# Windowed attention with sink keys, then a gated feed-forward: an early order written out by hand, sink values by a one-hot matmul, w_in loaded in mixed blocks, and output stores on another queue

## The chip, the cores and the metric

The kernel runs on one core of one Trainium2 chip. The metric is device time in microseconds, from the start to the end of one execution. Five engines run side by side, each through its own list of instructions: PE (matrix products), DVE (vector), ACT (activations), POOL (general purpose) and SP (here a queue that only issues transfers). They wait for each other on semaphores.

## The reference

The computation is attention in which each query sees the first 4 keys and the last 128 keys up to itself, and then a two-layer feed-forward with a gate. B = 4, H = 8, S = 768, D = 64; 3072 tokens, d_model 512, d_ff 2048; all inputs and the output are float32.

```python
scores = scale * np.matmul(q, k.transpose(0, 1, 3, 2))
keep = (pos[None, :] < 4) | ((rel >= 0) & (rel < 128))
scores = np.where(keep, scores, -1000000000.0)
a = np.exp(scores - np.max(scores, axis=-1, keepdims=True))
a = a / (np.sum(a, axis=-1, keepdims=True) + 1e-09)
x = np.matmul(a, v)                # heads side by side: 3072 x 512
h = x @ w_in                       # 3072 x 2048
g = h * (1.0 / (1.0 + np.exp(-beta * h)))
return g @ w_out                   # 3072 x 512
```

## The kernel before

**Tiling.** The tokens are cut into eight half-sequences of 384 tokens (`hb`, also `T_` in the feed-forward). Each has four units (`u`), a unit being two heads. The kernel computes in bf16 with float32 sums in the eight PSUM banks. For a half-sequence the stages are:

- loads of q, k (L510) and v into staging tiles, and casts to bf16 (`cast`, L530, through `copies`, L440 to L451: L444 on ACT, L446 on POOL, L449 on DVE);
- `T(u)`, L594: six transposes of q and k on PE (L602) into one bank, and one copy to `qkT`. From the fourth half-sequence on (`CUT` = 3) this is done by a transposing DMA (`XP`, L581);
- `SC(n)`, L657: scores of one or two tiles (L678), exponentials on ACT (L690, 128 x 1024), and masks in place on the tile `E`: L703 on POOL for the triangles, L698 on POOL or DVE for those with sink columns. `SS` (L716) computes scores against the sink keys;
- `AV(u)`, L736: products with the values (L757) and with the sink values `vS` (L746), reciprocal and scaling on DVE (L761, L763);
- `OT(u)`, L769: transposes of the result (L783) into `xT`; from `CUT` on by DMA (L777);
- `HQ(T_, m)`, L793: four matmuls with `w_in` for one of 16 column blocks of d_ff (L801), tanh on ACT (L806), gate on DVE (L808) into `g`;
- `OQ(T_, t, j)`, L815: matmuls with `w_out` for 128 tokens, 4 of the 16 blocks at a time (L821); after j = 3 the sum is copied to `osb` (L444 or L450) and stored by a DMA that SP issues (L830).

**Sink values.** `load_first` (L552) reads the first four value rows of every head with four small DMAs into `vS32`; `first_values` (L557) multiplies them with the ownership tile `own` into `vS`, one for each batch (L560).

**Weights.** `load_w(j)` (L512) loads 512 KB blocks j = 0 to 15, the first eight of w_in. A block of w_in holds 512 columns and half of the 512 rows, so a product of `HQ` needs two blocks. Blocks go through six staging slots, three of which lie in the third `g` buffer.

**Order.** `_program` builds a list of operations with their dependencies. `arrange` (L124) then plans it: it keeps a clock for each engine and always takes the operation that can start first. A group of PE instructions may pass at most two earlier ones (`SKIP` = 3). Operations with several possible engines (`any_of`) are given to the one that ends first. `resolve` puts semaphore waits where operations on different engines depend on each other. So each engine's list is fixed before the launch, and a late operation holds up all that stands behind it in the same list. The first half-sequence's order is written out (L965 to L1008), with fill matmuls on constants (L1003) where PE would otherwise stand idle; from L1009 a loop picks the next stage by what is ready first. Loads are listed in `LOADS` (L844): half-sequences 0 and 1, then all 16 weight blocks, then the others. SP issues all transfers, loads, transposes and stores, in one list.

Of the kernel before, what the change touches and what calls it, by code (L numbers as in the profile page):

```python
# [17 lines left out]
HALF = S // 2  # L18
# [4 lines left out]
class Op:  # L23
    __slots__ = ("eng", "fn", "deps", "signal", "count", "waits", "sem", "vc", "dma", "seq", "end", "ns", "alts",
                 "group", "tail", "hold", "preds", "ready", "left", "succ", "at")


class Graph:
# [7 lines left out]
    SKIP = 3  # L36
    SLACK = 0
# [16 lines left out]
    def add(self, eng, fn, ns=0, r=(), w=(), x=(), dma=None, alts=None, after=(), hold=550):  # L54
# [7 lines left out]
        o.signal, o.count, o.waits, o.vc, o.hold = False, 0, [], None, hold  # L62
# [61 lines left out]
    def arrange(self):  # L124
# [7 lines left out]
        for o in ops:  # L132
            for p in o.preds:
                p.succ.append(o)
        after = None
# [18 lines left out]
        def done(o):  # L154
            planned.add(id(o))
            new.append(o)
            for s in o.succ:
                s.left -= 1
                if s.left == 0 and s.eng != "pe":
                    pool.append(s)  # L160

        pool = [o for o in ops if o.left == 0 and o.eng != "pe"]
        while todo_pe or pool:
            best = None
            for i, grp in enumerate(todo_pe[:self.SKIP]):
# [182 lines left out]
def _program(nc, G, sb, ps, q, k, v, w_in, w_out, beta, out):  # L348
# [8 lines left out]
    maskS = sb("maskS", (128, 2, 128), BF16)  # L357
    beta_st = sb("beta_st", (16, 128), F32)
# [18 lines left out]
    vS32 = sb("vS32", (128, B, D), F32)  # L377
# [12 lines left out]
    def add(eng, fn, ns, r=(), w=(), x=(), dma=None, after=(), hold=550):  # L390
        return G.add(eng, fn, ns, r, w, x, dma, None, after, hold)
# [26 lines left out]
    held = {7}  # L418

    def choose(n):  # L420

        runs = [list(range(i, i + n)) for i in range(9 - n) if not held & set(range(i, i + n))]
        return min(((max(G.bank_at(("B", j)) for j in c), c) for c in runs), default=None)
# [8 lines left out]
    def take(n):  # L432
        got = choose(n)[1]
# [20 lines left out]
    def consts():  # L454
# [4 lines left out]
                                            base=0, channel_multiplier=-1), 150, r=["ones"], w=["ident32"])  # L459
        for i, sg in ((0, -1), (1, 1)):  # L460
# [7 lines left out]
        add("gp", lambda e: e.memset(vS32[:, :, :], 0.0), 250, w=["vS32z"])  # L468
# [7 lines left out]
        for i, sg in ((0, 1), (1, -1)):  # L476
            add("gp", lambda e, i=i, sg=sg: e.affine_select(
                maskS[:, i, :], ones[:, :], [[sg, 128]], ALU.is_ge, 0.0, base=min(sg, 0), channel_multiplier=-sg),
                250, r=["ones"], w=[("maskS0", i)])
        add("gp", lambda e: e.affine_select(maskS[:, :, :], maskS[:, :, :], [[0, 2], [0, 128]], ALU.is_ge, 1.0,  # L480
                                            base=-NSINK, channel_multiplier=1), 400,
            r=[("maskS0", 0), ("maskS0", 1)], w=["maskS"])
# [14 lines left out]
    def load(hb, n, i):  # L497

        b, t0, z = hb // 2, hb % 2 * HALF, hb % NSTG
        if n == "v" or hb >= CUT:  # L500
            src = {"q": q, "k": k, "v": v}[n][b, :, t0 + i * 128:t0 + (i + 1) * 128, :].rearrange("h p d -> p h d")
            dst, keys, ns = stg[n][z][:, i, :, :], [("stb", n, z, i)], 262144 / 240
        else:
            hs = slice(0, H) if i is None else slice(2 * i, 2 * i + 2)
# [565 lines left out]
```

## Time and profile before

| | |
|---|---|
| five executions | 230.63, 228.3, 231.03, 228.38, 231.51 us; median 230.63 |
| profiled execution: time, span | 230.63 us, 228.7 us |
| mean granted PE clock | 0.99 |
| longest instructions by group (busy us, mean ns) | L801 PE 95.1, 326; L821 PE 90.3, 379; L806 ACT 72.9, 585; L808 DVE 68.7, 550; L703 POOL 49.5, 717; L690 ACT 43.0, 1030 |
| SP, queue time of the four sink-value loads | 2.98 us, from 8.68 to 11.66 |
| SP waiting for the osb copy before a store | 31.3 us in 6 waits |
| a store, from issue to landing | 2.5 us median |
| moved by DMA in stretches of 5 us from 0 to 30 | 159, 267, 150, 324, 223, 291 GB/s |

The span is what the profile shows from the first to the last instruction; the rest of the time lies around it. Matmuls are pipelined, so their mean durations overlap: four matmuls of L801 follow each other in 0.65 us, four of L821 in 0.86 us. A line of the profile's groups gives the line of the kernel, the engine, the operation, its output and inputs, the count, then busy time and mean duration, then the idle time of that engine just before and what ended it.

### The profile page before, as it was taken

To read this page: it belongs to the slowest core of one execution; us is meant where nothing else is said; L and a number is where in the kernel's file an instruction comes from. 1 tells how busy PE (TensorE), PEld (TensorE's weight loads), DVE (VectorE), ACT (ScalarE), POOL (GpSimd) and SP (SyncE) were. 2 spreads that over 40 slices of the span, in tenths; PEclk is the share of its full clock that TensorE was granted. 3 is DMA by queue.
4 is the path that set the end of the run, shared out by engine and by line. 5 is a ranking of instruction groups with operands and counts; after the bars stand their busy time and mean duration, and the time that the engine had idled before them with its cause. 6 is when DMAs were issued, how large, how long until landed. Compare 5 with 4: busy or idle time off the path is not lost.

```text
span 228.7 us, 4562 instructions
## 1 busy us (share of the span) xinstructions
PE 214.8 (94%) x1771; PEld 124.8 (55%) x1795; DVE 139.4 (61%) x293; ACT 142.8 (62%) x226; POOL 66.0 (29%) x118
## 2 busy tenths in 40 slices
PE   8974799999999999999999999999999999999993
PEld 6662566554546556555655555656555565555541
DVE  2793469997596447557966563767765654533310
ACT  3844988765871487737667479672767764744421
POOL 6573592003361053407100047350120740000000
PEclk9999799999999999999999999999999999999998
DMA  6979799999976995967746995998769523011112
GB/s 180 236 200 332 207 357 359 341 321 237 220 150 141 242 216 86 221 165 147 155 87 162 229 207 94 216 187 171 131 127 208 185 80 83 0 46 49 47 48 89
DMA packets 95157, 39.79 MB, mean 174 GB/s; under 512 B 81808, under 2 KB 87968, under 8 KB 95136
## 3 DMA queue, kind: packets, MB, share of 16 engines
q1 hardware_dynamic: 95136, 39.51, 72.7%
q8 instruction: 14, 0.23, 0.4%
q14 instruction: 7, 0.06, 0.1%
HBM read 27.30 MB, written 6.29 MB: 147 GB/s over the span
## 4 chain that ended last, share of the span: by engine, by line
PE 82%; DMA 6%; ACT 4%; DVE 2%; SPq 2%; POOL 1%; issue 1%
PE P L801 36%; PE P L821 35%; DMA k_stage<-in_k_dram 6%; PE P L757 4%; PE P L678 4%; ACT E L690 2%; PE P L746 1%; PE P L602 1%; SPq L554 1%; ACT qkT L444 1%; POOL E L703 1%; SPq L510 1%; DVE w_in L449 1%; DVE g L808 1%; PE P L783 1%
## 5 line engine op out<-in xcount | busy, mean ns | idle before, releaser
L806 ACT ACTIVATE t<-P,hbeta 128x384 f32<-128x384 f32 x128 | 72.9, 585 | 39.3 <-PE P L801 31.1
L808 DVE SCALAR_TENSOR_TENSOR g<-t,P 128x384 bf16<-128x384 f32 x128 | 68.7, 550 | 45.9 <-ACT t L806 42.8
L801 PE MATMUL P<-xT,w_in 128*128 128x384 bf16 x512 | 95.1, 326 | 0.7 <-ACT E L690 0.5
L821 PE MATMUL P<-w_out,g 128*128 128x512 bf16 x360 | 90.3, 379 | 1.7 <-issue 0.6
L703 POOL TENSOR_SCALAR_AFFINE_SELECT E<-E 128x512 bf16<-128x512 bf16 x72 | 49.5, 717 | 77.0 <-ACT E L690 76.8
L801 PEld LDWEIGHTS P<-xT,w_in 128*128 128x128 bf16 x512 | 48.3, 98 | 37.4 <-DVE w_in L449 0.9
L821 PEld LDWEIGHTS P<-w_out,g 128*128 128x128 bf16 x384 | 36.5, 98 | 36.4 <-DVE w_out L449 0.3
L690 ACT ACTIVATE E<-P 128x1024 bf16<-128x1024 f32 x44 | 43.0, 1030 | 10.0 <-PE P L678 9.7
L444 ACT ACTIVATE osb<-P 128x512 f32<-128x512 f32 x19 | 11.4, 599 | 20.3 <-PE P L821 19.6
L763 DVE TENSOR_TENSOR onorm<-P,rden 128x384 bf16<-128x384 f32 x32 | 17.8, 556 | 1.0
L757 PE MATMUL P<-vaug,E 128*128 128x65 bf16 x352 | 17.1, 193 | 0.2 <-POOL E L703 0.2
L757 PEld LDWEIGHTS P<-vaug,E 128*128 128x128 bf16 x352 | 15.6, 97 | 2.4 <-POOL E L703 0.3
L678 PE MATMUL P<-qkT 64*128 64x128 bf16 (+1 forms) x288 | 14.8, 235 | 0.7 <-ACT ES L720 0.4
L678 PEld LDWEIGHTS P<-qkT 64*128 64x128 bf16 x288 | 9.7, 96 | 8.3 <-issue 2.6
L746 PE MATMUL P<-vS,ES 128*128 128x130 bf16 x64 | 12.8, 220 | 1.4 <-DVE vS L560 1.0
L449 DVE CAST k<-k_stage 128x512 bf16<-128x512 f32 (+1 forms) x19 | 9.6, 510 | 6.0 <-DMA k_stage<-in_k_dram 6.0
L761 DVE RECIPROCAL rden<-P 128x6 f32<-128x6 f32 x32 | 6.0, 188 | 10.4 <-PE P L757 10.3
L449 DVE CAST vaug<-v_stage 128x512 bf16<-128x512 f32 x21 | 9.9, 476 | 3.6 <-DMA v_stage<-in_v_dram 3.3
L446 POOL TENSOR_SCALAR_AFFINE_SELECT q<-q_stage 128x512 bf16<-128x512 f32 x6 | 4.3, 730 | 25.3 <-DMA q_stage<-in_q_dram 25.2
L1003 PE MATMUL P<-ones 128*128 128x256 bf16 x54 | 9.5, 321 | 1.1 <-POOL ones L455 1.1
L444 ACT ACTIVATE qkT<-P 128x768 bf16<-128x768 bf16 x9 | 7.0, 810 | 5.4 <-PE P L602 5.4
L449 DVE CAST q<-q_stage 128x512 bf16<-128x512 f32 (+1 forms) x15 | 7.1, 473 | 5.3 <-DMA q_stage<-in_q_dram 5.3
(50 smaller groups left out, 94.7 us busy)
## 6 DMA issues: line engine op xcount, KB each, us to landing
v_stage<-in_v_dram SPq DMA_DIRECT2D x24, 256.0 KB, 4.6
out_dram<-osb SPq DMA_DIRECT2D x24, 256.0 KB, 2.5
q_stage<-in_q_dram SPq DMA_DIRECT2D x15, 256.0 KB, 4.8
k_stage<-in_k_dram SPq DMA_DIRECT2D x15, 256.0 KB, 4.9
wst<-in_moe_w_in_dram SPq DMA_DIRECT2D x5, 512.0 KB, 9.2
wst<-in_moe_w_out_dram SPq DMA_DIRECT2D x4, 512.0 KB, 4.6
g<-in_moe_w_out_dram SPq DMA_DIRECT2D x4, 512.0 KB, 5.2
q_stage<-in_q_dram SPq DMA_DIRECT2D x2, 768.0 KB, 6.0
```

The lines of the kernel that those rows point to most:

```text
L444: return lambda e: e.activation(dst, src, AF.Copy, bias=0.0, scale=scale)
L449: return lambda e: e.tensor_copy(dst, src)
L678: add("pe", lambda e, dst=dst, kt=kt, kc=kc, rows=rows, q0=q0, nq=nq, u=u: e.matmul(dst, kt[rows, kc:kc + 128], qkT[rows, u % NT, 0, q0:q0 ...
L690: add("act", lambda e, src=src, dst_=dst_: e.activation(dst_, src, AF.Exp, bias=0.0, scale=SCALE), act_ns(1024), w=[("E", z)] + [("m", z, ...
L703: add("gp", lambda e, dd=dd, sg=sg: e.affine_select(dd, dd, [[0, 4], [sg, 128]], ALU.is_ge, 0.0, base=min(sg, 0), channel_multiplier=-sg), ...
L746: add("pe", lambda e, m=m, c0=c0: e.matmul(A[:, c0:c0 + 2 * (D + 1)], ES[u // 4 % 2][:, m * 128:(m + 1) * 128], vS[b % 2][:, 2 * hp:2 * hp ...
L757: e.matmul(A[:, c0:c0 + D + 1], E[t_ % NE][:, i, hh, :], vaug[vz][:, kb % NK, 2 * hp + hh, :], start=a, stop=o, skip_group_check=True), 31,
L763: add("dve", lambda e: e.tensor_tensor(onorm[on][:, :, :, :].rearrange("p m h d -> p (m h) d"), av[:, :, 0:D], rden[on][:, :].unsqueeze(2) ...
L801: add("pe", lambda e, c=c: e.matmul(hp, w_in16[:, c, m * 128:(m + 1) * 128], xT[:, c, t0:t0 + HALF], start=(c == 0), stop=(c == 3)), mm_ns ...
L806: add("act", lambda e: e.activation(tt[ti][:, :], hp, AF.Tanh, bias=0.0, scale=hbeta[:, m:m + 1]), act_ns(HALF) + 93, r=["hbeta"], w=[("t" ...
L808: add("dve", lambda e: e.scalar_tensor_tensor(gt[T_ % NG][:, m, :], tt[ti][:, :], 1.0, hp, ALU.add, ALU.mult), dve_ns(HALF), r=[("t", ti)] ...
L821: add("pe", lambda e, m=m: e.matmul(P[:, bk, :], gt[T_ % NG][:, m, t * 128:(t + 1) * 128], w_out16[:, m, :], start=(m == 0), stop=(m == NM ...
```

## The change

- **Sink values.** For the first batch a matmul takes the place of the loads: a constant one-hot tile `sel` picks the first four rows of the first v block, for all heads (`first_values_pe`), and the multiplication with `own` then reads PSUM. For each later batch one DMA reads 16 rows of v (`load_first`), placed among the later loads.
- **w_in.** A block now holds 256 columns and all 512 rows, so one block serves two products of `HQ`. Weight blocks come before q and k of the second half-sequence: `LOADS` is half-sequence 0, w0, w1, w2, q, w3, k, w4, w5, v, then w6 to w15. The first casts are bound to an engine.
- **Loads of the first half-sequence.** q and k come in three transfers each in place of four. SP's order of the early loads is fixed by a chain. Beta is loaded behind w1.
- **The early order.** Transposes, scores, attention of the first half-sequence, then products H0 to H10 mixed with transposes and scores of the second, are written out with their PSUM banks. q and k of the first eight units get a bank and a copy each. PE groups may pass nine others while PE's planned time is under 60 us.
- **Masks.** The triangles of the first two half-sequences may also be applied by DVE, with `maskT`.
- **First output products.** For `T_` = 0 the order is j outside, t inside, with three banks held.
- **Stores.** All output stores but those of the last half-sequence are issued by POOL; the plan books 1000 ns of POOL for each.

```diff
+    WIDE, EARLY = 10, 60000
...
-            for i, grp in enumerate(todo_pe[:self.SKIP]):
+            for i, grp in enumerate(todo_pe[:self.SKIP if self.free["pe"] > self.EARLY else self.WIDE]):
...
-            src = w_in_src[:, 2 * h:2 * h + 2, m * 512:(m + 1) * 512]
+            src = w_in_src[:, :, j * 256:(j + 1) * 256]
...
+        any_of(copies(dst, src_, {"act": 947} if j == 0 else {"gp": 1060} if j < 3 else {"act": 947, "dve": 602, "gp": 1060}), r=[("wst", j % NWS)], w=[("w16", m, h)])
...
-        add("sp", lambda e: e.dma_start(vS32[s_:128:16, :, :], v[:, :, s_, :].rearrange("b h d -> h b d")), 60,
-            r=["vS32z"], w=[("vS32", s_)], dma=f"ds{s_}")
+        add("sp", lambda e: e.dma_start(vS32[:, 0, :], v[b, :, 0:16, :]), 100,
+            w=["vS32"], dma="ds")
...
+    def first_values_pe():
+        G.begin()
+        bk = take(1)
+        add("pe", lambda e: e.matmul(P[:, bk[0], :], sel[:, :], vaug[0][:, 0, :, 0:D], start=True, stop=True), mm_ns(512),
+            r=["sel", ("v", 0, 0)], x=[("B", bk[0])])
+        add("dve", lambda e: e.tensor_tensor(
+            vS[0][:, :, 0:D], P[:, bk[0], :].rearrange("p (h d) -> p h d", d=D),
+            own[:, :].unsqueeze(2).to_broadcast([128, H, D]), ALU.mult), dve_ns(H * D),
+            r=["own", ("vSo", 0)], w=[("vS", 0)], x=[("B", bk[0])])
+        give(bk)
...
-        bs = take(1)
+        bs = take(1) + (take(1) if hb < 2 else [])
...
+        if len(bs) == 2:
+            for i in range(2):
+                mp = P[:, bs[i], :].bitcast(BF16)[:, i * HALF:(i + 1) * HALF]
+                any_of(copies(qkT[:, u % NT, i, :].rearrange("p (s j) -> p s j", j=NK),
+                              mp.rearrange("p (j s) -> p s j", j=NK), {"dve": 470, "act": 380}),
+                       w=[("qkT", u % NT, i, c) for c in range(NK)], x=[("B", bs[i])])
...
+                    if TILES[t_][0][1] < 8:
+                        alts["dve"] = (lambda e, dd=dd, tri=tri: e.tensor_tensor(dd, dd, tri, ALU.mult), 335)
...
-            add("sp", lambda e: e.dma_start(out_t[3 * T_ + t], osb[z][:, :]), 262144 / 300, r=[("osb", z)],
-                dma=f"do{z}")
+            eng = "gp" if T_ < NSB - 1 else "sp"
+            add(eng, lambda e: e.dma_start(out_t[3 * T_ + t], osb[z][:, :]), 262144 / 300, r=[("osb", z)],
+                dma=f"do{eng}{z}", hold={"sp": 550, "gp": 1000, "act": 600}[eng])
...
-    LOADS = xl(0) + xl(1) + list(range(16)) + [x for hb in range(2, NSB) for x in xl(hb)]
+    x1 = xl(1)
+    LOADS = xl(0) + [0, 1, 2] + x1[:1] + [3] + x1[1:2] + [4, 5] + x1[2:] + list(range(6, 16))
+    LOADS += [("f", 1)] + [x for hb in range(2, NSB) for x in xl(hb) + ([("f", hb // 2 + 1)] if hb in (3, 5) else [])]
...
-    OS = [(T_, t, j) for T_ in range(NSB) for t in range(3) for j in range(4)]
+    OS = [(0, t, j) for j in range(4) for t in range(3)]
+    OS += [(T_, t, j) for T_ in range(1, NSB) for t in range(3) for j in range(4)]
...
+    for x in "T0 T1 S0 T2 S1 T3 S4 S2 V S3".split():
+        if x == "V":
+            cast(0, "v", 0)
+            first_values_pe()
+        else:
+            {"T": T, "S": SC}[x[0]](int(x[1:]))
...
+    for name, i in [("A", 0), ("A", 1), ("R", 0), ("A", 2), ("R", 1), ("A", 3), ("R", 2), ("R", 3)]:
+        step(name, i)
...
+    early = "H0 H1 H2 H3 H4 H5 T4 T5 T6 T7 H6 S5 H7 H8 S6 H9 S7 H10".split()
+    for x in early:
+        if x == "H0":
+            beta_in()
...
+        step(x[0], int(x[1:]))
```

In this code "A" stands for `AV`, "R" for `OT`, "H" for `HQ`, "S" for `SC` and "gp" for POOL.

## The prediction

> **What bounds the kernel now.** I read the busy shares first, then the span in slices, the windows by stage, the timeline of the first 30 us, the chain of waits, and last the queues of POOL and SP.
>
> ```profile
> PE 214.8 (94%) x1771; PEld 124.8 (55%) x1795; DVE 139.4 (61%) x293; ACT 142.8 (62%) x226; POOL 66.0 (29%) x118
> PE   8974799999999999999999999999999999999993
> POOL 6573592003361053407100047350120740000000
> ```
>
> PE is the bound; the row of tenths shows that it is full from the sixth slice (28.6 us) to the last. So only the front can give much. Windows over the whole program, then over the fill matmuls of L1003 alone (start:end, length, PE busy, then the other engines):
>
> ```profile
> 0.00:4.40 4.40, 3.35 (x16) 2.34 (x17) 0.64 (x2) 1.49 (x2) 3.45 (x22) 1.00 0.50 147
> 4.40:18.90 14.50, 12.37 (x157) 8.82 (x155) 12.05 (x26) 8.89 (x12) 8.13 (x13) 1.00 0.91 239
> 18.90:28.40 9.50, 5.68 (x71) 3.89 (x68) 3.31 (x7) 6.55 (x10) 4.08 (x6) 0.82 0.91 255
> 28.40:35.00 6.60, 5.98 (x72) 4.05 (x73) 4.44 (x10) 5.55 (x10) 6.60 (x10) 1.00 1.03 360
> 35.00:60.00 25.00, 24.30 (x171) 14.25 (x171) 22.54 (x46) 17.97 (x34) 2.79 (x6) 1.00 1.05 303
> ...
> sum 28.40, PE 9.48 PEld 5.61; mean PE 3.16 PEld 1.87
> ```
>
> Up to 28.4 PE is busy 21.4 us, 9.5 of them filler: only 11.9 us are work, 16.5 us are not. Between 35 and 190 it idles 0.70 + 0.31 + 0.48 + 0.79 = 2.3 us. What the front waits for is in the chain of waits in order of time, and on PE's timeline:
>
> ```profile
> 9.17 0.57 SPq L554
> 12.19 9.15 DMA k_stage<-in_k_dram
> 15.00 0.22 PE L746 MATMUL P<-vS,ES 128*128 128x130 bf16 x1 [1.01 <-DVE vS L560]
> 18.73 0.34 PE L783 MATMUL P<-ident,onorm 128*128 128x128 bf16 x3
> 21.85 0.75 PE L602 MATMUL P<-ident,k 128*128 128x128 bf16 x3 [2.61 <-DVE k L449]
> 28.48 1.47 PE L801 MATMUL P<-xT,w_in 128*128 128x384 bf16 x8 [0.52 <-ACT E L690]
> ```
>
> Four sink-value loads hold SP at 8.7 to 11.7; the second half-sequence's k is issued behind them and takes 9.15 us; PE stands still for it; the first product with w_in starts at 28.48, though the last transpose of its input was done near 19.1.
>
> **The early order.** Three steps bring the first xT forward. (a) The sink rows come through a one-hot matmul from v's first block (at the price of the 512-column matmul in the chain, 0.86 us for 4: 0.2 us) instead of DMAs; the 1.01 us wait at 15.00 goes. (b) DVE ran L560 twice there (2.15 us, 13.74 to 15.89), the second for another batch, ahead of the first reciprocal at 15.81; that second 1.1 us goes to a later place, and about 0.5 us with it. (c) q and k of each unit get two PSUM banks: one ACT copy of 810 ns becomes two of about 485 (ACT's 384-column xT copy), +0.16 us of engine time for each of eight units, beside other work. So xT is ready at 19.1 - 1.5 = 17.6 us. The two small operations for the one-hot tile add 0.45 us to POOL at the start and a memset of 0.30 goes; POOL has about 2 us free at 4 to 6. What is late next is w_in.
>
> SP queue: the 2.98 us of L554 and beta's 0.47 go from the front, eight q/k loads become six (1.0 us less). Loads for the sink rows of later batches return as one DMA each (about 0.5 us of SP), after the weights. Beta's load stands behind the second w_in load; its transpose (0.23 us PE, 0.17 us DVE) now stands just before the first tanh, which waits if beta is late; it has some 8 us to land and took 3.4.
>
> Data: ahead of the third w_in load lie 2.36 + 1.57 = 3.9 MB. By the stretches of 5 us, before had moved 0.80, 2.13, 2.88, 4.50, 5.62, 7.07 MB at 5, 10, ... 30 us. It had moved 3.9 MB by 18.2, with a hole at 10 to 15 (150 GB/s) that closes when L554 goes. One w_in load now serves two products of 0.65 us (16 matmuls in 2.60 us), so products H0 to H5 can run from 17.6 to 21.5. Only the first is sure to find its weights early; a miss costs under 1 us. Their casts are now bound to engines: the first to ACT (0.63 for half as many columns: about 1.1), two to POOL (1.05 each), both with idle time at 15 to 21. While PE is in its first 60 us, a group that is ready may pass up to nine others in place of two, so H6 and H7 can come forward into the gap before k. The row length of a w_in load falls from 2 KB to 1 KB, which no row here shows: below by nothing, above by the v loads' 256-byte rows (239 GB/s in the window where they run, against 360 from 28.4 on: 0.7 us for each of eight, 5.8 in all). I take nothing, as q's 768-byte rows make up most of the 324 GB/s at 15 to 20.
>
> Against it, three weight loads (1.57 MB) and w_in's fourth now precede k of the second half: 6.0 MB up to k. Hole closed, 5.1 MB at 20 us and then 0.31 MB per us: 23 us, against 21.3 (earliest 22; without the gain 26.4). That half's chain is 1.7 us later.
>
> Gain by that limit: eleven products, 11 x 0.65 = 7.15 us of PE work, done in time idle before, less 1.7: 5.4 us. A second limit is ACT: each product wants one L806 (0.585), and the six exponentials (1.03 each) have no other engine. From 17.6 to 35 ACT was busy 12.7 us (0.6, then 6.55 and 5.55 in the two windows), idle 4.7. The split copies put 4 x 0.485 on it for the second half's units in place of 3 x 0.81: 0.5 freed. Leave 1.7 for the gap between H7's end (22.8) and the first copy behind k (24.5): (4.7 + 0.5 - 1.7) / 0.585 = 6 products more than before by 35, 3.9 us of PE. This one ends last: I take 3.9, between 2 and 6.5.
>
> The rest of the front: masks of the first two halves may go to DVE (0.40 us on L698, against 0.72 on POOL). At 28.4 to 35 POOL is full and PE idles 0.62; I take 0.4 gained. The T_=0 output products in the order j outside, t inside hold three banks in place of one; the next scores, which want five of eight, come near 60 us. Nothing, covered by that order; if it failed, a score burst would wait for 3 x 0.86 us.
>
> **The stores.** 21 of 24 leave SP for POOL. On SP L830 costs 0.56 us each and waits 31.3 us; behind it stand loads and both DMA transposes. But PE idles only 2.3 us in 35 to 190, so the freed queue is worth 0 to 1: nothing, nearest to the rows of PE waits, which hardly name these transfers. On POOL each store waits for its osb copy, and queued behind are the masks, for which L757 waits. POOL is busy 41.0 of 130 us between 60 and 190:
>
> ```profile
> L703 POOL TENSOR_SCALAR_AFFINE_SELECT E<-E 128x512 bf16<-128x512 bf16 x54 | 36.3, 701 | 73.9 <-ACT E L690 73.7
> L757 PE MATMUL P<-vaug,E 128*128 128x65 bf16 x352 | 17.1, 193 | 0.2 <-POOL E L703 0.2
> ```
>
> A POOL store's issue is not in the trace: nearest row SP's (0.56, longest 1.42); the kernel's own plan books 1.0 for it; the Trainium skill, "DMA: Bandwidth & Descriptors", section Specifications, puts the first byte at about 1 us. I take 1.0: 21 us of POOL, 62 of 130. PE's wait for masks, 0.5 us now with the loads before it, may double: 0.5 us of loss, between -1 (freed SP) and 8.
>
> Here a rule speaks against the change. In the trace POOL's masks run 632 ns at best and 1085 at worst, DVE's casts 416 and 853: the two engines hold each other up by at most 0.45 us. "SBUF — State Buffer", section "A bandwidth-pool intuition that's wrong (but worth ruling out)", says that a DMA issued by GpSimd is held until the DVE copy ends, about 3100 ns in place of 620. DVE casts from SBUF fill 18.3 of the 130 us (14%), so three stores meet one: by the rule 3 x 2.5 = 7.5 us on POOL, a third of it (POOL's busy share) on PE, 2.5 us; by the row 3 x 0.45 / 3 = 0.5. I take the row, which fits casts of 0.43 us.
>
> Sum: -3.9 - 0.4 + 0.2 (sink matmul) + 0.5 = -3.6 us. The profiled execution took 230.63 us (span 228.7 and 1.9 around it), which is also the median of the five runs: 227.0.
>
> **The rivals.**
> - *The front is bound by its transfers.* DMA is at 0.91 to 1.05 in the windows from 4.4 to 60 us, and the order only permutes the same 13.1 MB (4.7 of q, k, v, 8.4 of weights). If k lands at 26.4, 7.15 - 5.1 = 2.0 us are gained, and the 1 KB rows can eat that: 228.6 to 231, say 230. Against it: the hole at 10 to 15.
> - *Stores on POOL hold the masks.* At 60 to 190 masks come in bursts of 2.4 us. If each store that meets a busy POOL (32%) passes its 1.0 + 0.43 us to PE, less 0.2 of planned slack, 21 x 0.32 x 1.23 = 8.3 us: 227.0 - 0.5 + 8.3 = 234.8, slower. It decides from 4.1 + 2.3 = 6.4 us, or 0.30 us a store. For it: POOL E L703 is in the chain at 105.9. Against: one such wait in 130 us.
> - *The front fills fully.* If DVE takes more copies and ACT is no limit, 6.5 us in place of 3.9: 224.4.
>
> **How the numbers follow.** Two us or so (1%) can't be told from no change; the five runs lie between 228.3 and 231.5. The likeliest case 0.52 (224.5 to 229.3, of which 0.06 within 1%), front fully filled 0.11, transfer-bound 0.20 (within 1%), masks held 0.17. Faster 0.57, same 0.26, slower 0.17. The range 222.5 to 231.5 leaves out the held masks and little below.
>
> **What would show it.** L801 starting near 17.6; the first k of the second half landing near 23; ACT nearly full from 24 to 35; PE idle small after. L703 waiting for stores, or L757 for L703 more than 1 us in all, would show the masks held. I am wrong if w_in is late at 17.6, or if POOL's stores take over 1.5 us each.

## The result and the profile after

| | before | after |
|---|---|---|
| median | 229.69 us (227.41 to 232.83, 80 runs) | 228.61 us (226.89 to 230.35, 43 runs) |
| profiled execution: time, span, granted clock | 230.63, 228.7 us, 0.990 | 228.21, 226.3 us, 0.998 |

The ratio of after to before is 0.9965, with the interval [0.9947, 0.9983]: about 0.8 us faster, where 3.6 were forecast. (Medians are of all runs; the ratios leave out runs more than 1.5% above the fastest of their kernel.) The two profiled executions differ by 2.4 us, more than the medians do; the profile of before fell on a run with a lower clock. So the profiles serve here for the where, the ratios for the how much.

The page of after, busy shares and the rows of tenths:

```profile
PE 213.8 (94%) x1762; PEld 122.4 (54%) x1787; DVE 141.3 (62%) x299; ACT 147.0 (65%) x237; POOL 71.3 (32%) x131
...
PE   8797978999999999999999999999999999999994
...
POOL 6263154016350266047000564073100570000000
```

PE's hole at the third to fifth slice (7, 4, 7 before) is nearly gone (9, 7, 9), and a shallow dent (7, 8) has come behind it, at 28 to 40 us. Windows of after, with the same columns as before:

```profile
4.40:18.90 14.50, 11.70 (x146) 7.93 (x143) 10.44 (x25) 9.93 (x16) 6.78 (x12) 1.00 0.97 279
18.90:28.40 9.50, 8.66 (x66) 4.71 (x64) 7.61 (x17) 8.24 (x18) 1.32 (x2) 1.00 1.05 320
28.40:35.00 6.60, 5.04 (x83) 3.21 (x82) 6.49 (x13) 6.48 (x9) 3.50 (x5) 1.00 0.94 289
35.00:60.00 25.00, 23.94 (x184) 13.87 (x185) 20.51 (x42) 15.32 (x26) 6.99 (x12) 1.00 1.10 312
```

From 18.9 to 28.4 PE is busy 8.66 us, none of it filler, in place of 5.68. From 28.4 to 35 it idles 1.56 us in place of 0.62, with ACT (6.48 of 6.60) and DVE (6.49) full; from 35 to 60 it idles 1.06 in place of 0.70.

To see when work is won and lost, I count the matmuls of each kind up to a time, weigh each with its spacing in a burst (0.16 us for one of `HQ`, 0.22 for one of `OQ`, and so on) and take the difference to before. I call it the lead. Some matmul records are missing, so it is good to about half a us, and it drifts later.

| lead over before, us, at | 20 | 25 | 30 | 35 | 40 | 45 | 60 |
|---|---|---|---|---|---|---|---|
| after | 0.1 | 3.1 | 3.9 | 2.6 | 0.7 | 1.0 | 1.6 |

The 3.9 us that were forecast for the early order are there at 30 us, and 3.2 of them are gone at 40. PE's timeline of after shows the stretch (start, length, instruction, and in brackets the idle time before and what ended it):

```profile
19.61 5.96 PE L860 MATMUL P<-xT,w_in 128*128 128x384 bf16 x32
25.40 0.33 PE L649 MATMUL P<-ident,q 128*128 128x128 bf16 x3
...
28.42 0.62 PE L733 MATMUL P<-qkT 64*128 64x256 bf16 x14
...
30.99 0.39 PE L733 MATMUL P<-qkT 64*128 64x256 bf16 x6 [0.52 <-ACT E L745]
31.90 0.40 PE L733 MATMUL P<-qkT 64*128 64x128 bf16 x8 [0.52 <-ACT E L745]
32.81 0.40 PE L733 MATMUL P<-qkT 64*128 64x256 bf16 x6 [0.52 <-ACT E L745]
...
38.70 0.82 PE L860 MATMUL P<-xT,w_in 128*128 128x384 bf16 x4 [0.59 <-DVE g L867]
```

Eight products run back to back from 19.61 (28.48 before). Then come the transposes of the second half-sequence, at 25.40 (the first of k at 21.85 before), since its k landed late, as POOL's timeline shows:

```profile
24.68 0.66 POOL L473 TENSOR_SCALAR_AFFINE_SELECT k<-k_stage 128x512 bf16<-128x512 f32 x1 [2.91 <-DMA k_stage<-in_k_dram]
```

From 30 us PE is paced by ACT: each group of scores waits until an exponential frees its banks. ACT's timeline of after, and then of before:

```profile
28.52 0.58 ACT L865 ACTIVATE t<-P,hbeta 128x384 f32<-128x384 f32 x1 [0.29 <-PE P L860]
29.00 3.76 ACT L745 ACTIVATE E<-P 128x1024 bf16<-128x1024 f32 x4
32.62 0.52 ACT L779 ACTIVATE ES<-P 128x384 bf16<-128x384 f32 x1
32.99 0.62 ACT L865 ACTIVATE t<-P,hbeta 128x384 f32<-128x384 f32 x1
33.45 1.99 ACT L745 ACTIVATE E<-P 128x1024 bf16<-128x1024 f32 x2
```

```profile
25.18 1.03 ACT L690 ACTIVATE E<-P 128x1024 bf16<-128x1024 f32 x1
26.09 0.51 ACT L720 ACTIVATE ES<-P 128x384 bf16<-128x384 f32 x1
26.46 4.72 ACT L690 ACTIVATE E<-P 128x1024 bf16<-128x1024 f32 x5
```

The second half's six exponentials end at 35.4 in place of 31.2. Its masks, values and transposes all follow later by about as much, and until then PE has little else, since most of the early products are behind it: from 30 to 40 us it idles 2.5 us (0.5 before).

The stores, from the groups of after (see the prediction for the same rows of before):

```profile
L759 POOL TENSOR_SCALAR_AFFINE_SELECT E<-E 128x512 bf16<-128x512 bf16 x64 | 42.9, 692 | 61.3 <-ACT E L745 60.8
L890 POOL DMA_DIRECT2D out_dram<-osb x21 | 12.1, 579 | 51.7 <-ACT osb L471 51.7
L816 PE MATMUL P<-vaug,E 128*128 128x65 bf16 x352 | 17.2, 193 | 1.5 <-DVE E L753 0.7 <-DVE E L763 0.3 <-POOL E L759 0.3
```

A store costs POOL 0.58 us (at most 0.78). Masks on POOL wait for exponentials, not for stores, and PE waited 0.3 us for a POOL mask.

### The profile page after: what moved, and what is told of

It reads as the page before. It is cut to its first block, busy times and chain, and to the rows that moved or that the text cites. A ratio compares the mean times of both kernels' runs of the same rounds, so it can differ in the third digit from the quotient of the medians.

```text
span 226.3 us, 4534 instructions
## 1 busy us (share of the span) xinstructions
PE 213.8 (94%) x1762; PEld 122.4 (54%) x1787; DVE 141.3 (62%) x299; ACT 147.0 (65%) x237; POOL 71.3 (32%) x131
## 4 chain that ended last, share of the span: by engine, by line
PE 76%; DVE 11%; ACT 4%; DMA 3%; POOL 1%; issue 1%; SPq 1%
PE P L880 34%; PE P L860 33%; PE P L816 4%; PE P L733 3%; DMA k_stage<-in_k_dram 3%; ACT E L745 3%; DVE g L867 2%; DVE E L763 2%; PE P L805 1%; DVE vaug L476 1%; DVE onorm L822 1%; DVE E L753 1%; DVE w_in L476 1%; POOL E L759 1%; SPq L541 1%
## 5 line engine op out<-in xcount | busy, mean ns | idle before, releaser
L865 ACT ACTIVATE t<-P,hbeta 128x384 f32<-128x384 f32 x128 | 73.9, 583 | 47.9 <-PE P L860 42.3
L867 DVE SCALAR_TENSOR_TENSOR g<-t,P 128x384 bf16<-128x384 f32 x128 | 70.1, 551 | 48.5 <-ACT t L865 45.0
L860 PE MATMUL P<-xT,w_in 128*128 128x384 bf16 x512 | 96.6, 326 | 0.9 <-DVE g L867 0.6
L759 POOL TENSOR_SCALAR_AFFINE_SELECT E<-E 128x512 bf16<-128x512 bf16 x64 | 42.9, 692 | 61.3 <-ACT E L745 60.8
L890 POOL DMA_DIRECT2D out_dram<-osb x21 | 12.1, 579 | 51.7 <-ACT osb L471 51.7
L471 ACT ACTIVATE osb<-P 128x512 f32<-128x512 f32 x21 | 12.6, 598 | 13.7 <-PE P L880 13.7
L753 DVE TENSOR_TENSOR E<-E,maskS 128x512 bf16<-128x512 bf16 x16 | 9.3, 588 | 5.1 <-ACT E L745 5.1
L1071 PE MATMUL P<-ones 128*128 128x256 bf16 x45 | 8.7, 342 | 1.1 <-POOL ones L482 1.1
L476 DVE CAST vaug<-v_stage 128x512 bf16<-128x512 f32 x18 | 8.9, 496 | 0.0
```

The lines of the kernel that those rows point to most:

```text
L471: return lambda e: e.activation(dst, src, AF.Copy, bias=0.0, scale=scale)
L476: return lambda e: e.tensor_copy(dst, src)
L759: alts = {"gp": (lambda e, dd=dd, sg=sg: e.affine_select(dd, dd, [[0, 4], [sg, 128]], ALU.is_ge, 0.0, base=min(sg, 0), channel_multiplier= ...
L860: add("pe", lambda e, c=c: e.matmul(hp, w_in16[:, c, m * 128:(m + 1) * 128], xT[:, c, t0:t0 + HALF], start=(c == 0), stop=(c == 3)), mm_ns ...
L865: add("act", lambda e: e.activation(tt[ti][:, :], hp, AF.Tanh, bias=0.0, scale=hbeta[:, m:m + 1]), act_ns(HALF) + 93, r=["hbeta"], w=[("t" ...
L867: add("dve", lambda e: e.scalar_tensor_tensor(gt[T_ % NG][:, m, :], tt[ti][:, :], 1.0, hp, ALU.add, ALU.mult), dve_ns(HALF), r=[("t", ti)] ...
```

## The experiments

The candidates were: that the stores on POOL took the gain; that k of the second half comes too late behind three weight loads; that DVE is full of masks; that q and k in three transfers hold up the first half; that the old gap in PE's work brings a lower clock, and filling it is what pays; and later, that ACT, DVE or the late beta is the limit at 30 to 40 us. Each ratio below is to runs of before taken beside it, with 6 to 22 runs of each kernel tried. The kernels of e1, e9, e10 and e5 keep the planned order; the others are planned anew, which can shift work elsewhere.

The PE clock that is granted in a run matters too: runs in which it dips are longer (see the last section). So the tables also give the median of those runs alone whose mean clock was 0.997 or more, with their number. For before that is 228.4 us (104 runs, 228.3 to 228.6 in each measurement). This column was worked out afterwards and has no interval.

**Parts of the change alone.**

Stores back on SP, all else kept (`e1_stores_on_sp`):

```diff
-    G.arrange()
+    G.arrange(); [setattr(o, "eng", "sp") for o in G.ops if o.dma and o.dma.startswith("dogp")]
```

> The changed kernel, with its plan kept (PE, DVE, ACT in the same order) and its 21 stores emitted by SP at the planned places. Theory 1 (the early gain of 4 us is given back between 30 and 40 us, where the second half's attention runs late; stores cost nothing): the same as the changed kernel, 0.995 to 0.998 of before, and the same PE work done at 30 and 40 us. Theory 2 (stores on POOL took the gain): some 3 us faster than the changed kernel, 0.983 to 0.986. Against both: slower than the changed kernel by 1 us or more, if SP's list needs to be free of stores.

Only the stores on POOL, in the kernel before (`e6_before_pool_stores`):

```diff
-            add("sp", lambda e: e.dma_start(out_t[3 * T_ + t], osb[z][:, :]), 262144 / 300, r=[("osb", z)],
-                dma=f"do{z}")
+            eng = "gp" if T_ < NSB - 1 else "sp"
+            add(eng, lambda e: e.dma_start(out_t[3 * T_ + t], osb[z][:, :]), 262144 / 300, r=[("osb", z)],
+                dma=f"do{eng}{z}", hold={"sp": 550, "gp": 1000}[eng])
```

> The kernel before with the stores of all but the last half-sequence issued by POOL, nothing else of the change (the planner makes its own order after it). Theory 1 and 4 (stores are worth nothing either way): 0.997 to 1.003 of before. Theory 2 (they cost some 3 us): 1.010 to 1.016. If a free SP list is worth something: 0.990 to 0.996.

Only the one-hot matmul for the sink values, in the kernel before (`e7_before_sink_matmul`), and then both of these (`e12_sink_pool_stores`, whose diff is the sum):

```diff
...
-    LOADS = xl(0) + xl(1) + list(range(16)) + [x for hb in range(2, NSB) for x in xl(hb)]
+    LOADS = xl(0) + xl(1) + list(range(16)) + [("f", 1)] + [x for hb in range(2, NSB) for x in xl(hb) + ([("f", hb // 2 + 1)] if hb in (3, 5) else [])]
...
-        if n_ == 10:
-            for s_ in range(NSINK):
-                load_first(s_)
...
-    for c in range(NK):
-        cast(0, "v", c)
+    cast(0, "v", 0)
+    first_values_pe()
+    cast(0, "v", 1)
+    cast(0, "v", 2)
```

> The kernel before with one part of the change alone: the sink values by the one-hot matmul and one later DMA for each other batch. It takes the 2.98 us of four small loads out of SP's list ahead of the second half's q and k. Theory 1 (what counts at the front is when the second half's attention gets k): k lands near 18.5 in place of 21.3, PE's gap before it nearly closes, the lead in PE work at 40 us is 2 us or more and is kept: 0.986 to 0.993, better than the whole change. Rival (the first product needs the early weights, so this part alone gives little): 0.995 to 0.999.

> The kernel before with the sink values by the one-hot matmul (alone 1.002, with a lead of 2.3 us at 40 us that was lost again, 1.2 us of it at 170 to 190 us, where a v load and transposes stood behind stores in SP's list) and the stores on POOL. If the stores in SP's list are what takes the lead back late: 0.989 to 0.994. If the lead is lost for other reasons (the planner's new order, PE's clock): 0.998 to 1.003.

| kernel | median, us | ratio, interval | clock 0.997 and up, us (runs) | lead at 30, 40 us |
|---|---|---|---|---|
| after | 228.61 | 0.9965 [0.9947, 0.9983] | 228.3 (23) | 3.9, 0.7 |
| e1: all but the stores | 229.36 | 0.9992 [0.9963, 1.002] | 228.8 (12) | 3.9, 0.9 |
| e6: only the stores | 229.53 | 0.9978 [0.9948, 1.0009] | 227.7 (7) | (low clock at 20 to 35) |
| e7: only the sink matmul | 229.77 | 1.0022 [0.9987, 1.0057] | 229.4 (9) | 2.2, 2.3 |
| e12: sink matmul and stores | 227.72 | 0.9953 [0.9927, 0.9978] | 227.5 (14) | 2.7, 2.8 |

The stores on POOL take nothing: e6 is not slower than before, and after is not slower than e1. Rather, everything but the stores (e1) brings nothing measurable. And the two small parts by themselves, in the old order of loads and work, do about as well as the whole change by the ratio, and better among the runs at the full clock, where after is not told from before. e7 missed both of its forecasts and e12 lies between its two.

What the stores cost on SP is seen late in e1, where PE is busy 14.3 of 15 us at 170 to 185 (14.9 in after). SP's timeline, then DVE's:

```profile
169.32 2.57 SPq L632 DMA_TRANSPOSE qkT<-q  x2
171.94 2.20 SPq L541 DMA_DIRECT2D v_stage<-in_v_dram  x3
174.18 7.04 SPq L890 DMA_DIRECT2D out_dram<-osb  x2
```

```profile
175.46 0.43 DVE L476 CAST vaug<-v_stage 128x512 bf16<-128x512 f32 x1 [2.64 <-DMA v_stage<-in_v_dram]
```

In SP's one list the last v loads stand behind transposes, and between these stood three stores at 150.1, 158.2 and 160.9 us. They were issued at 171.9, in after at 167.9. DVE's next instruction is a cast of that v; it waits 2.64 us, a gate stands behind it, and a score group on PE waits 0.57 us for the gate. In e7 the same place costs more: PE is busy 13.3 of 15 us there (14.7 in e12). A store stands in SP's list behind transposes until 172.18, so ACT's copy of the next sum into `osb` waits for it, and scores on PE wait for the copy:

```profile
174.64 0.60 ACT L445 ACTIVATE osb<-P 128x512 f32<-128x512 f32 x1 [1.23 <-DMA out_dram<-osb]
```

```profile
175.29 0.35 PE L732 MATMUL P<-qkT,kS 128*32 128x384 bf16 x4 [0.43 <-ACT osb L445]
```

That fits e7's lead of 2.3 at 40 us ending in no gain, and e12's lasting. It is not shown to be all of it: e7 and e12 are planned anew, and before, with its stores on SP too, is busy 14.7 of the same 15 us.

e12 also shows the other order at the front. PE's timeline:

```profile
18.58 0.74 PE L618 MATMUL P<-ident,k 128*128 128x128 bf16 x3 [0.76 <-DVE k L450]
...
20.26 0.79 PE L694 MATMUL P<-qkT 64*128 64x256 bf16 x14
...
22.55 0.82 PE L817 MATMUL P<-xT,w_in 128*128 128x384 bf16 x4 [0.58 <-ACT E L706]
```

Without the four sink-value DMAs, and with k ahead of the weights, the second half's k is transposed at 18.58 and its first scores run at 20.26 (28.42 in after). The first product comes at 22.55, three us later than in after, and the lead at 30 us is 2.7 in place of 3.9. But nothing is given back.

**What takes the lead at 30 to 40 us.** k of the second half ahead of the third w_in load (`e2_k_before_w2`); q and k of the first half in four transfers (`e4_four_loads`); both (`e8_k_early_four_loads`):

```diff
-    LOADS = xl(0) + [0, 1, 2] + x1[:1] + [3] + x1[1:2] + [4, 5] + x1[2:] + list(range(6, 16))
+    LOADS = xl(0) + [0, 1] + x1[:2] + [2, 3, 4, 5] + x1[2:] + list(range(6, 16))
```

```diff
-            hs = slice(0, H) if i is None else slice(2 * i, 2 * i + 2) if i < 2 else slice(4, H)
+            hs = slice(0, H) if i is None else slice(2 * i, 2 * i + 2)
...
-        return [(0, n, i) for i in range(3) for n in "qk"] + [(0, "v", c) for c in range(NK)]
+        return [(0, n, i) for i in range(4) for n in "qk"] + [(0, "v", c) for c in range(NK)]
...
```

> The changed kernel with q and k of the second half loaded ahead of the third and fourth w_in blocks (1.05 MB earlier for k). Theory 1: k lands some 3 us earlier than 24.7 (near 21.5), the second half's scores start near 25.5 in place of 28.4, the lead in PE work at 40 us rises from 0.7 to 2 or 3 us, and the time falls by 1 to 2 us: 0.988 to 0.993 of before. Theory 2 (stores): no change, 0.995 to 0.998. Theory 3 (DVE is full from 25 to 45 by the masks it took over): little, 0.994 to 0.998.

> The changed kernel with q and k of the first half in four transfers each, two heads in each, as before. The third unit's transposes waited for k at 10.4 us, 2.3 us later than before. If the transfer of four heads is what holds them, they come near 9, the first product with w_in starts near 18.3 in place of 19.6, and, by theory 1, little of that is kept, since k of the second half is two issues (1 us) later: 0.993 to 0.998 of before. If the start alone counts: 0.990 to 0.993.

> The changed kernel with both edits that helped alone: q and k of the second half ahead of the third w_in block (0.992), and four transfers each for q and k of the first half (0.992). If they act on two different waits in one chain (first half's transposes, then the second half's k), they add up in part: 0.985 to 0.990. If both only feed the stretch of 30 to 40 us where ACT runs the exponentials back to back, no more than one of them: 0.991 to 0.994.

Triangle masks on POOL only (`e3_masks_on_pool`: the condition `< 8` becomes `< 0`):

> The changed kernel with the triangle masks of the first two half-sequences on POOL alone, as in the kernel before. Theory 3: DVE falls below full at 30 to 40 us, the lead at 40 us rises by 1 us or more, 0.989 to 0.993 of before. Theory 1 (the late k and the exponentials on ACT set that stretch): within 0.3% of the changed kernel, 0.994 to 0.999, as the exponentials stay back to back.

More work on one engine, the orders kept. On ACT (`e9_act_more`), three of the second half's exponentials run a second time into a buffer that is free then; on DVE (`e10_dve_more`), four casts of w_in do (`extra` is set for blocks 3 to 6):

```diff
-            add("act", lambda e, src=src, dst_=dst_: e.activation(dst_, src, AF.Exp, bias=0.0, scale=SCALE),
...
+            two_ = (t_ - 5) // 2 if t_ in (5, 7, 9) else None; add("act", lambda e, src=src, dst_=dst_, two_=two_: [e.activation(o_, src, AF.Exp, bias=0.0, scale=SCALE) for o_ in ([] if two_ is None else [osb[two_][:, :].bitcast(BF16).rearrange("p (s h w) -> p h s w", s=4, h=2)]) + [dst_]][-1],
...
```

```diff
-    def copies(dst, src, ns, scale=1.0):
+    def copies(dst, src, ns, scale=1.0, extra=[]):
...
-                return lambda e: e.tensor_copy(dst, src)
+                return lambda e: [e.tensor_copy(o_, src) for o_ in extra + [dst]][-1]
...
```

> The changed kernel, every order kept, with three of the second half's six exponentials run once more into unused room (3 x 0.92 = 2.8 us more on ACT between 29 and 34 us). If ACT sets the end of the front (theory 1), 2 to 2.8 us are added to the time of the changed kernel: 1.005 to 1.009 of before. If DVE sets it (theory 3), ACT has room behind it: less than 1 us, 0.997 to 1.001.

> The changed kernel, every order kept, with the DVE casts of four w_in blocks run once more into unused room (4 x 0.68 = 2.7 us more on DVE between 22 and 35 us). If DVE sets the end of the front (theory 3): 2 to 2.7 us more, 1.005 to 1.008 of before. If ACT does (theory 1): less than 1 us more, 0.997 to 1.001. If both are in the chain in turn: 1 to 2 us more in both runs.

| kernel | median, us | ratio, interval | clock 0.997 and up, us (runs) | first product at | lead at 30, 40 us |
|---|---|---|---|---|---|
| after | 228.61 | 0.9965 [0.9947, 0.9983] | 228.3 (23) | 19.61 | 3.9, 0.7 |
| e2: k earlier | 227.48 | 0.9923 [0.989, 0.9956] | 227.1 (15) | 18.66 | 4.6, 2.0 |
| e4: four transfers | 227.54 | 0.9922 [0.9896, 0.9947] | 227.5 (12) | 17.77 | 4.2, 1.0 |
| e8: both | 227.64 | 0.99 [0.9858, 0.9941] | 227.6 (2) | 18.00 | 5.3, 1.7 |
| e3: masks on POOL | 229.2 | 0.9964 [0.9931, 0.9996] | 228.5 (7) | | |
| e9: ACT +2.8 us | 231.03 | 1.0074 [1.0045, 1.0103] | (0) | | |
| e10: DVE +2.7 us | 230.12 | 1.0028 [1.0001, 1.0054] | 230.1 (9) | | |

An earlier k pays 0.0042 of the time, about 1.0 us, and four transfers as much, both at the edge of the intervals; together they are not told apart from either alone. e4 went against the theory that little of an earlier start is kept. (Its one profile does not show its gain at 40 us, so where it comes from stays argued.)

Work added to ACT comes out as (1.0074 / 0.9965 - 1) x 228.6 = 2.5 of 2.8 us, work added to DVE as 1.4 of 2.7. So both engines count in that stretch, but which counts more is not shown, as the clock has a share in it: in e9's profile it dips before the added work begins (0.68 at 20 to 25 us) and again at 35 to 40 us, and none of e9's 17 runs kept it at 0.997. Among the runs between 0.9905 and 0.997 after has 229.1 us (21 runs), e10 230.1 (8) and e9 230.7 (7); that is 1.1 us for DVE and 1.6 for ACT, across different measurements.

The masks are not the cause. This is e3 in the window of the loss:

```profile
30.00:35.00 5.00, 3.03 (x39) 1.93 (x40) 2.20 (x4) 5.00 (x8) 4.57 (x7) 0.90 0.91 292
```

DVE falls to 2.20 of 5 us (4.95 in after), and PE is no better off, since ACT is still full at 5.00.

**The clock.** 22 more fill matmuls in the gap of the kernel before, its orders unchanged (`e5_before_fill`):

```diff
-                        self.filler = (self.WARM, self.filler[1])
+                        self.filler = (self.WARM if grp[0].group <= self.fill_to - 4 else 65, self.filler[1])
...
```

> The kernel before, every engine's order kept, with 22 more fill matmuls on PE ahead of the second half's first transposes, where PE stood still for 2.6 us and the granted clock fell to 0.76 and 0.90 in the next 10 us. Theory 4 (the executions of the kernel before differ by that fall of the clock: of 75, those with a mean clock of 0.997 and more took 228.3 us at the median, those under 0.9905 took 230.8): nearly all executions keep the full clock, and the median falls to about 228.3: 0.994 to 0.997 of before, with no earlier work at all. If the clock is no cause but only goes with something else: no change, 0.998 to 1.003; if the fill delays the transposes: slower, up to 1.003 to 1.006.

Measured: 230.3 us, ratio 1.0042 [1.0014, 1.007], the branch in which the fill delays the transposes. In its profile the first cast of k begins at 19.66 us, but the transposes wait until the fill ends, at 21.72; and the dip of the clock comes at 28 to 31 us instead. At a mean clock of 0.997 and up e5 takes 229.8 us (14 of its 22 runs), before beside it 228.4 (25 of 51). So filling the gap does not pay; what before would gain without the dip was not tested.

**With k early, what is next?** In e8 PE stands still for beta, whose load had come behind q and k. PE's timeline of e8:

```profile
21.23 0.23 PE L520 MATMUL P<-ident,beta_st 16*128 16x16 f32 x1 [0.85 <-DMA beta_st<-in_moe_beta_dram]
```

ACT's first tanh is at 21.70 there, 3.7 us behind the first product. Three edits on e8: casts of w_in and of the second half on POOL and DVE in place of ACT (`e11_casts_on_pool`); beta ahead of the first w_in load (`e13_beta_first`); both (`e15_beta_casts_pool`). And on e13, the exponentials earlier in the list (`e14_exps_first`):

```diff
-        any_of(copies(dst, src_, {"act": 947} if j == 0 else {"gp": 1060} if j < 3 else {"act": 947, "dve": 602, "gp": 1060}), r=[("wst", j % NWS)], w=[("w16", m, h)])
+        any_of(copies(dst, src_, {"act": 947} if j == 0 else {"gp": 1060} if j < 6 else {"act": 947, "dve": 602, "gp": 1060}), r=[("wst", j % NWS)], w=[("w16", m, h)])
...
-        ns = {"act": 413, "dve": 400} if hb == 0 and n != "v" else {"act": 540, "dve": 340, "gp": 612}
+        ns = {"act": 413, "dve": 400} if hb == 0 and n != "v" else {"dve": 340, "gp": 612} if hb == 1 else {"act": 540, "dve": 340, "gp": 612}
```

```diff
-        if x == 2:
+        if x == 0:
```

```diff
-    early = "H0 H1 H2 H3 H4 H5 T4 T5 T6 T7 H6 S5 H7 H8 S6 H9 S7 H10".split()
+    early = "H0 H1 H2 H3 T4 T5 T6 T7 S5 S6 S7 H4 H5 H6 H7 H8 H9 H10".split()
```

> The kernel with k ahead of the third w_in block and four transfers for the first half (0.990), with work taken from ACT and DVE in the front: the casts of w_in blocks 3 to 5 bound to POOL, which is free for 8 of 10 us at 20 to 30, and no q or k cast of the second half on ACT (2 x 0.62 us). If ACT's and DVE's load at 20 to 38 us is what gives the early lead back, 0.5 to 1.5 us less: 0.984 to 0.988 of before. If it is the chain of exponentials alone, which starts no earlier: 0.988 to 0.992.

> The kernel of e8 (k of the second half early, four loads of q and k), with beta's load issued ahead of the first w_in block. In e8 ACT stood idle for 3.38 us until beta had landed (first tanh at 21.38). Theory A: that idle time is what takes 3 us of the lead back between 30 and 40 us, since ACT then has its tanhs and the second half's exponentials in one list; then the lead at 40 us rises from 1.7 to 3 or more and the ratio to before is 0.980 to 0.987. Theory B: the scores and exponentials of the second half end as late as before whatever the tanhs do, because they wait for k and their own chain: ratio 0.987 to 0.993, lead at 40 us 1.5 to 2.3.

> The kernel of e13, with the early list changed: after H0 to H3 the transposes T4 to T7 and the scores S5 to S7, then H4 to H10. Theory A (tanhs in front of and between the exponentials on ACT delay the second half's attention): its scores end earlier, AV of the second half starts 1 us or more earlier, lead at 40 us 1 us above that of e13, ratio 0.978 to 0.986. Theory B (what is saved on one side is lost on the other: PE waits for k with H4 to H7 not yet allowed): lead at 25 us lower by 2 us, ratio as e13 or up to 0.008 above it.

> The kernel of e11 (e8 with six of the first w_in casts off ACT and DVE) with beta's load issued ahead of the first w_in block. If ACT was held by beta and by casts together, the lead at 40 us is 3 or more and the ratio 0.978 to 0.985, below that of e13; if casts play no part, as e13 within 0.002.

Then, on e13, work taken from DVE: the second half's triangle masks (`e16_beta_masks_pool`: `< 8` becomes `< 4`), its four casts of v (`e17_beta_v_pool`, below), both (`e18_beta_both_pool`):

```diff
+        if n == "v" and hb == 1:
+            ns = {"gp": 612}
         any_of(copies(dst, src, ns), r=r, w=w)
```

> The kernel of e13, with the triangle masks of the second half-sequence on POOL alone. In e13 ACT has 2.7 us free between 30 and 40 us, DVE is busy 9.9 of 10, POOL 4.3, and PE waits for DVE (gates, casts, masks). Theory A (with ACT relieved, DVE is the next limit): DVE falls by about 2 us in 25 to 40 us, PE's waits there by 1 us or more, ratio 0.980 to 0.986. Theory B (the masks go from a full DVE to a POOL that takes 0.7 in place of 0.43 for each, the same end): ratio 0.987 to 0.993, as e13.

> The kernel of e13, with the four casts of the second half-sequence's v (0.43 each on DVE) on POOL, which is idle there. Theory A (DVE is the next limit): ratio 0.982 to 0.987, and the PE waits for DVE's cast of v (0.6 at 31) are gone. Theory B: as e13, 0.987 to 0.992.

> Both edits of e16 and e17. Theory A: DVE relieved by some 4 us between 25 and 40 us, lead at 40 us 3.5 or more, ratio 0.978 to 0.985. Theory B: POOL becomes the limit there or the gain is none: 0.987 to 0.995.

| kernel | median, us | ratio, interval | clock 0.997 and up, us (runs) | lead at 30, 40 us |
|---|---|---|---|---|
| e11: e8, casts off ACT | 227.56 | 0.9897 [0.987, 0.9923] | 227.1 (12) | 4.8, 1.5 |
| e13: e8, beta first | 227.08 | 0.9886 [0.9837, 0.9935] | 226.1 (3) | 5.0, 2.8 |
| e15: e11, beta first | 226.81 | 0.9894 [0.9843, 0.9945] | 226.3 (4) | 5.2, 3.5 |
| e14: e13, exponentials first | 228.01 | 0.9933 [0.9903, 0.9964] | 227.5 (11) | 4.8, 2.4 |
| e16: e13, masks on POOL | 229.1 | 0.9984 [0.996, 1.0008] | 228.3 (9) | 5.3, 3.3 |
| e17: e13, v casts on POOL | 226.75 | 0.9882 [0.984, 0.9924] | 226.6 (5) | 5.2, 1.6 |
| e18: both | 231.48 | 1.0084 [1.0045, 1.0123] | (0) | 5.1, 3.2 |

Beta first takes ACT out of the way, as the windows of e13 show:

```profile
30.00:35.00 5.00, 3.33 (x65) 2.63 (x66) 4.97 (x10) 4.66 (x7) 4.32 (x5) 1.00 0.96 327
35.00:40.00 5.00, 4.28 (x38) 2.42 (x36) 4.90 (x13) 2.60 (x4) 0.00 (x0) 1.00 1.05 407
```

ACT is busy 7.3 of 10 us, DVE 9.9, and PE still idles 2.4; the longest waits in PE's timeline there are for DVE (a cast of v, a gate):

```profile
31.10 0.27 PE L816 MATMUL P<-vaug,E 128*128 128x65 bf16 x3 [0.56 <-DVE vaug L476]
...
33.02 0.23 PE L805 MATMUL P<-vS,ES 128*128 128x130 bf16 x1 [1.11 <-DVE g L867]
```

The lead at 40 us is 1 us higher than e8's, but a part of that is the clock: the profiles of e8, e11 and e17 have 0.71 to 0.84 at 35 to 40 us. By the ratio, too, beta's share is not told apart from nothing. e14 was a miss: a lower lead at 40 us and a ratio no better, so running the exponentials ahead of the tanhs does not help. e11 and e15 against e8 and e13 show no gain from moving the casts. Nor does e17; but DVE stays as full as in e13 there (9.9 of 10 us at 30 to 40), so it did not relieve DVE.

e16 and e18 were meant to name DVE as the next limit and do not. Their lead at 40 us is 0.4 to 0.5 above e13's, within the error of that count, and yet they are 1% and 2% slower. The reason in e16 lies far from the edit, at 90 to 100 us:

```profile
90.00:100.00 10.00, 7.25 (x72) 3.58 (x73) 8.20 (x14) 6.95 (x10) 5.56 (x8) 1.00 0.85 162
```

PE idles 2.75 us there, where e13 idles nothing: the planner, starting from other times, put three groups of scores behind each other with no product between. They wait 0.28, 0.52 and 0.52 us for exponentials, and the next output product but one waits 1.18 us for a gate. e18 loses in the same place (PE is busy 7.11 of 10 us at 90 to 100). So whether DVE is the next limit stays open, and e16 and e18 measure a replanned middle, not masks.

What beats both kernels: e17, e13, e15, e11 and e8 all lie at 0.988 to 0.990, 1% under before, with intervals that overlap.

## Why the prediction came out as it did

The range (222.5 to 231.5) holds 228.6, and the sign was right. The size was not: 0.8 us in place of 3.6. And the sign was luck: what was to bring the gain brought nothing that can be measured (e1), and what there is goes with the stores, which were booked as a loss, or with fewer dips of the clock. Neither sign of being wrong that the prediction named came: no product waited for w_in at the start, and no store took POOL over 1.5 us. Of what it expected to see, "PE idle small after" failed.

- **The early order, 3.9 us: the term that failed.** It was the ACT limit, "6 products more than before by 35, 3.9 us of PE". Measured alone with the other front parts (e1) it is 0.0008 of the time, 0.2 us [-0.5, 0.8]. The products were done early (lead 3.9 at 30 us), so the first half of the step stands. What failed is that a lead by 35 us was booked as time saved at the end. A product done early is worth something only if PE has other work at the time from which it was taken. For the late k the forecast left 1.7 us of ACT idle, but it still counted the six exponentials as done by 35 us and put what follows them at nothing. They ended at 35.4 in place of 31.2, behind a k that landed at 24.65 in place of 21.3, and the second half's masks and values came later with them; PE then idled 2.5 us at 30 to 40 us (0.5 before), and 3.2 of the 3.9 us were gone. That the late k has a part is shown by e2, about 1.0 us; that ACT and DVE have one, by e9 and e10. The rest is not shown: e2, with its early k and no dip of the clock there, still falls from 4.6 to 2.0 us.
- **k at 23.** The bytes moved by 20 us were right (5.1 MB). But when k landed, 0.8 MB more had gone than the 6.0 MB up to it (6.81 MB in after), and in before some 0.9 MB: bytes of loads that were issued behind it. A landing time reckoned from the bytes ahead alone was too early here.
- **xT ready at 17.6, first product there.** It was 19.61. The SP time of the sink values was freed as forecast. But the third transfer of q and k now holds four heads: k of unit 2 landed 6.50 us after its issue, and its transposes began at 10.36 (8.08 before). The prediction counted six loads in place of eight as 1.0 us of SP saved, and not that half the heads now wait for the larger one. With four transfers (e4) the first product is at 17.77.
- **Masks on DVE, 0.4 us.** None seen: e3 without them is at 0.9964, the change at 0.9965; the intervals (0.7 us and more) could hide 0.4.
- **Sink matmul, 0.2 us of loss.** It was costed as a matmul. What it frees in SP's list brings k forward instead (transposed at 18.58 in e12): with the stores moved too it carries a gain of the size of the whole change's, alone (e7) none.
- **Stores on POOL, 0.5 us of loss.** Each took 0.58 us in place of 1.0, and PE waited 0.3 us for masks. By e6 they gain 0.5 us [-0.2, 1.2], by after against e1 0.6; neither is clear of nothing alone, but with e12 against e7 they point the same way. So "the freed queue is worth 0 to 1: nothing" was probably the wrong end of its own bounds. SP's list matters at 170 to 185 us, where a late v load holds DVE; PE's wait rows name the gate there, not the transfer. The rival with masks held fell.
- **The row against the rule of the Trainium skill's "SBUF — State Buffer".** The row was right to take. A store's issue at most 0.78 us (median 0.56) leaves no room for issues held for some 3 us. By its section "A bandwidth-pool intuition that's wrong (but worth ruling out)" the hold ends with the DVE copy, so with casts of 0.43 us the 2.5 us a store were more than the rule makes of this case. Whether a cast held up any store's transfer no run here shows.
- **The transfer-bound rival, 230.** Its number is near, and the order of loads has a part (e2). But k landed at 24.65, not 26.4, and what PE waited for last there was ACT behind it.

Not shown: what takes 2 us of e13's lead between 30 and 40 us, and what of the change's other parts (mixed blocks, wider passing, j outside t) does anything; these were not tried singly.

## What to carry to other kernels

Work that is pulled forward into an idle stretch shortens the program only if the engine has other work where it used to stand. Before booking a gain, list what remains for that engine behind it, and when that becomes ready; here the loads for the early work went ahead of the load on which the next stage hung. And in a kernel whose lists are planned as a whole, a local edit can lose 1% elsewhere: look at the whole span before blaming the edit.

## What the runs showed of the hardware

- **The granted clock goes with the time from run to run.** Of 75 runs of the kernel before that were measured with e1 to e4, 32 had a mean clock of 0.997 or more and a median of 228.3 us, 25 between 0.9905 and 0.997 with 229.9, and 18 below that with 230.8. The dips are short and deep: the clock is 0.50 at 23 to 26 us in the profile of before, at 28 to 31 in e5's, and at 20 to 23 and 37 to 40 in e9's; with its two dips e9's mean is 0.985, with one before's is 0.990. Of 44 runs of after, 23 have the full clock and a median of 228.3, 21 the middle one and 229.1, none the lowest. So at the full clock the change is not told from before, and its gain may be fewer dips. This split was made afterwards. With the gap filled (e5) the dip came later, behind 24 to 28 us, where PE is busy 2.3 of 4 us; what brings the dips stays open.
- **A store issued by POOL** took 0.58 us of that engine and landed after 2.9 us (median), against 2.5 in before from SP.
- **ACT stands behind one transfer.** In after the first exponential came 1.6 us later than before (9.05 for 7.44); most of it is a q cast ahead of it in ACT's list, for whose DMA ACT stood idle 1.41 us.
